# A kernel of linear attention and a mixture of experts: the experts' token lists built by products of one-hot matrices in place of scatters to DRAM

## The chip, the cores and the metric

The kernel runs on one core of one Trainium2 chip. A core has TensorE (PE, matrix products; the load of a weight tile is shown as PEld), VectorE (DVE), ScalarE (ACT), GpSimd (POOL) and SyncE (SP), each with its own instruction stream, and 16 DMA engines that all queues share. The metric is the device time of one execution in microseconds (us), less is better. The three executions of the kernel before took 561.39, 561.18 and 560.62 us, so the median is 561.18 us. The profile is of a further execution that took 574.06 us.

## What is computed

First a delta-rule attention over 768 steps for 4 x 8 heads of 48 features, then a router that sends each of the 3072 tokens to one of 8 experts, a two-layer network each.

```python
for t in range(S):
    kt, vt, bt = (k_n[:, :, t], v[:, :, t], beta[:, :, t, None])
    y[:, :, t] = np.einsum('bhd,bhde->bhe', q[:, :, t], state)
    v_old = np.einsum('bhde,bhd->bhe', state, kt)
    state = state + bt[:, :, :, None] * np.einsum('bhd,bhe->bhde', kt, vt - v_old)
...
logits = x @ w_gate
expert_idx = np.argmax(logits, axis=1)
...
gate_w = probs[np.arange(N), expert_idx]
...
for e in range(E):
    lo, hi = (boundaries[e], boundaries[e + 1])
    h = np.maximum(x_sorted[lo:hi] @ w1[e], 0.0)
    y_sorted[lo:hi] = h @ w2[e]
y = y_sorted[inv_perm]
return (gate_w[:, None] * y).astype(np.float32)
```

Here x is the attention's output, 3072 rows of 384, and the hidden width is 1024. All is in float32.

## The kernel before

**The turns.** The 768 steps are cut into 12 turns of 64 steps. A turn is a chain between PE and ACT: the old state goes through the keys (L558), the residual R is copied out of PSUM, two triangular inverses are applied (L587) with a product across between them (L597), each followed by a copy on ACT, then the state is updated (L611) and copied to S, which starts the next turn. DVE computes the inverses ahead (L441 to L521) and is the busiest engine in the first seven turns. Each turn gives 256 rows of x: `output` (L643) and `logits` (L663, L673, L682) run a turn behind the chain, and x goes to DRAM as `xs`.

**Routing.** The 24 tiles of 128 tokens are handled in five groups: 8, 8, 2, 4 and 2 tiles. `route(m, 0)` finds each token's expert, `route(m, 1)` its rank among that expert's tokens (products with a triangle and with ones, L736 and L740), and from rank and expert a place in a list, `ri`. The entry `ent` is a pair: the token's number (L766) and its gate. For every tile of tokens one indirect DMA of GpSimd (L770) then writes 128 entries of 8 bytes to their places in one of two lists in DRAM, which alternate; both were filled with a large number by two DMAs of 194 KB at about 34 us. There are 24 such scatters.

**Reading the lists.** After groups 0 to 2, that is 18 tiles, the first 256 tokens of expert 0 are known. `early_rows` reads their entries back (`both_e`, L968 takes the minimum of the two lists, L837 makes integers `rows_ei`) and GpSimd gathers the rows from `xs` (L840), while the last two turns still run. `early` then computes these 256 rows: transposes L900, first layer L918, second layer L947, after the last turn. After group 4, `entries` reads the rest (six DMAs on SP to `both_l`, L866 takes the minimum, L837 makes `rows_i`), and the gathers of all experts follow from it. The 10 DMAs that load the weights of experts 1 and 2 stand behind these six on SP's queue.

**The order.** A planner in Python (class `Plan`) holds a cost, a priority and dependencies for each step, simulates the engines, and so writes one fixed order for each engine. Its `prio` numbers only order the plan; at run time an instruction waits for the data that it reads or overwrites. The planner also puts fillers into PE's idle time (L1084, products with the identity)[...]. Each queue works strictly in its order: what stands behind a waiting instruction waits too.

**The experts.** From about 281 us on, PE goes through the 8 experts with hardly a break (L900, L918, L947), the weights of three experts in a ring (`blkA`, `pA`), and GpSimd scatters the finished rows to the output (L847).

Of the kernel before, what the change touches and what calls it, by code (L numbers as in the profile page):

```python
# [20 lines left out]
NT = S // C  # L21
# [17 lines left out]
OUT, LOG = 0.6, 0.9  # L39
LATER, OUTL = 7, 1.1  # L40
# [149 lines left out]
def _consts():  # L190

    p = np.arange(128)[:, None]
    j = np.arange(128)[None, :]
    rev = np.broadcast_to(E - np.arange(E), (128, E))
    first = np.broadcast_to(np.arange(E), (128, E))
    closed = first + E * EARLY * (first == 0)
    i = np.arange(32)[None, :]
    q = np.arange(64)[None, :]  # L200
    parts = [
        ("rev", rev), ("first", first), ("upper", E * (p < j)), ("ones", np.full((128, 128), E)),
        ("ident", p == j), ("number", p),
        ("later", np.concatenate([p % 64 < q, (p % 64) ^ 32 < q], axis=1)), ("fold", p % 32 == i),
        ("places", np.broadcast_to(E * (CAP + 128 * np.arange((NL - CAP) // 128)), (128, (NL - CAP) // 128))),
        ("closed", closed),
    ]
    at, where = 0, {}
    for name, a in parts:
        where[name] = (at, a.shape[1])  # L210
        at += a.shape[1]
    return np.concatenate([a for _, a in parts], axis=1).astype(np.float32), where
# [3 lines left out]
def tile_kernel(ctx: ExitStack, tc: tile.TileContext, kq, ktok, vtok, betal, wgk, w1, w2, out):  # L216
# [7 lines left out]
    lists = [nc.dram_tensor(f"lists{i}", (E * NL, 2), FP32, kind="Internal").ap() for i in range(2)]  # L224
# [113 lines left out]
    P.op("POOL", 0.6, lambda: nc.gpsimd.memset(empty[:], float(FAR)), w=["empty"], prio=-20)  # L338
    for i in range(2):
        P.op(  # L340
            "SP", 0.6, dma(nc.sync, lists[i].rearrange("(p s) o -> p (s o)", p=128), empty[:]),
            r=["empty"], w=[("lists", i)], prio=-1.1,
        )
# [351 lines left out]
    lgs = [pool.tile([128, TG, E], FP32, name=f"lg{i}") for i in range(2)]  # L695

    def route(m, part):
# [9 lines left out]
        ent, ri = w("ent", (TG, 2)), w("ri", (TG,), I32)  # L707
# [44 lines left out]
        else:  # L752
# [5 lines left out]
        dve(4, lambda: nc.vector.tensor_copy(out=ri[:, 0:n], in_=po[:, 0:n]), [K("po")], [K("ri")], pr)  # L758
# [4 lines left out]
        dve(4, lambda: nc.vector.reciprocal(out=ent[:, 0:n, 1], in_=su[:, 0:n]),  # L763
            [K("su")], [K("ent")], pr)
        for i, t in enumerate(g):
            dve(1, lambda i=i, t=t: nc.vector.tensor_scalar(  # L766
                out=ent[:, i, 0:1], in0=const("number"), scalar1=float(t * 128), scalar2=None,
                op0=OP.add), ["cf"], [K("ent")], pr)
        for i, t in enumerate(g):
            P.op("POOL", 1.0, lambda i=i: nc.gpsimd.indirect_dma_start(  # L770
                out=lists[i % 2], out_offset=bass.IndirectOffsetOnAxis(ap=ri[:, i : i + 1], axis=0),
                in_=ent[:, i, :], in_offset=None, bounds_check=E * NL - 1, oob_is_err=False),
                r=[K("ent"), K("ri")], w=[("lists", i % 2)], prio=pr, lat=2.0)
# [31 lines left out]


    LAST = 3 * E
    both_l = pool.tile([128, 2, LAST + 1 + E, 2], FP32, name="both_l")
    rows = pool.tile([128, LAST + 1 + E, 2], FP32, name="rows")
    rows_i = pool.tile([128, LAST + 1 + E], I32, name="rows_i")  # L810
    both_e = pool.tile([128, 2, 2, 2], FP32, name="both_e")
    rows_e = pool.tile([128, 2, 2], FP32, name="rows_e")
# [15 lines left out]
    def prepare(i):  # L828
        v, k = XIN[i]
        P.op("POOL", 1.4, lambda v=v: nc.gpsimd.memset(v, 0.0),  # L830
             w=k + [("xin", i, t) for t in range(4)], prio=10 if i else 9.5)
        if i:
            return
        dve(2 * (LAST + 1 + E) * 2, lambda: nc.vector.memset(both_l[:], float(FAR)), [], [("both", i, j) for i in range(2) for j in range(3)], 9)

    def ids(o, i, k):
        P.op("DVE", 0.12, lambda: nc.vector.tensor_copy(out=o, in_=i), r=[k], w=[k + "i"], prio=12.4)  # L837
# [14 lines left out]
    def by_place(i):  # L852
        return lists[i].rearrange("(n e) o -> n e o", e=E)

    def entries():

        for i in range(2):
            e, q = nc.sync, "SP"
            late = by_place(i)[EARLY : EARLY + 128, 0:1, :]
            P.op(q, 0.3, dma(e, both_l[:, i, LAST : LAST + 1, :], late), r=[("lists", i)], w=[("both", i, 0)], prio=12.3, lat=2.5)  # L860
            tiles = lists[i][0 : 384 * E].rearrange("(p x) o -> p x o", p=128)
            rest = by_place(i)[384:CAP]

            P.op(q, 0.3, dma(e, both_l[:, i, 0:LAST, :], tiles), r=[("lists", i)], w=[("both", i, 1)], prio=12.3, lat=2.5)
            P.op(q, 0.3, dma(e, both_l[0:32, i, LAST + 1 :, :], rest), r=[("lists", i)], w=[("both", i, 2)], prio=12.3, lat=2.5)
        P.op("DVE", 0.13, lambda: nc.vector.tensor_tensor(  # L866
            out=rows[:], in0=both_l[:, 0], in1=both_l[:, 1], op=OP.min),
            r=[("both", i, j) for i in range(2) for j in range(3)], w=["rows"], prio=12.4)
        ids(rows_i[:], rows[:, :, 0], "rows")

    def place(e, t):

        return LAST + 1 + e if t == 3 else LAST if e == 0 else t * E + e

    def fetch(e):
        xv = XIN[e % 2][0]
        allx = [("xs", t) for t in range(2 * NT)]
        for t in (3, 2) if e == 0 else range(4):
            n, c = 32 if t == 3 else 128, place(e, t)
            P.op("POOL", 1.0, lambda t=t, n=n, c=c: gather(xv[0:n, t * DM : t * DM + DM], rows_i[0:n, c : c + 1]),  # L880
                 r=["rowsi", *allx], w=[("xin", e % 2, t)], prio=30 + e, lat=2.5)
# [48 lines left out]
    def finish(on_dve, b, n, gate, idx, k, p):  # L930
# [8 lines left out]
             r=[("bk", b), k], w=[ky], prio=p)  # L939
        P.op("POOL", 1.0, lambda: scatter(y[0:n], idx), r=[ky, k + "i"], w=["out"], prio=p, lat=2.5)  # L940
# [19 lines left out]
    def early_rows():  # L960

        weights(0, 8)
        prepare(0)
        for i in range(2):
            e, q = nc.gpsimd, "POOL"
            P.op(q, 1.0, dma(e, both_e[:, i], lists[i][0 : EARLY * E].rearrange("(p t e) o -> p t e o", t=2, e=E)[:, :, 0, :]),
                 r=[("lists", i)], w=[("both_e", i)], prio=10, lat=2.5)
        P.op("DVE", 0.13, lambda: nc.vector.tensor_tensor(  # L968
            out=rows_e[:], in0=both_e[:, 0], in1=both_e[:, 1], op=OP.min),
            r=[("both_e", 0), ("both_e", 1)], w=["rows_e"], prio=10.5)  # L970
        ids(rows_ei[:], rows_e[:, :, 0], "rows_e")
        xv = XIN[0][0]
        for t in range(2):
            P.op("POOL", 1.0, lambda t=t: gather(xv[:, t * DM : t * DM + DM], rows_ei[:, t : t + 1]),
                 r=["rows_ei"] + [("xs", i) for i in range(18)], w=[("xin", 0, t)], prio=11, lat=2.5)

    def early():
        xT, hT = parts(0, EARLY, 0)
        guard = [k for i in range(3) for k in kKQ(i)]
        turned_rows(0, (0, 1), xT, 20.5, guard)  # L980
        hidden(0, xT, hT, 21, guard, (0, 1, 4, 5))
        for t in range(2):
            second(0, t, hT, 128 * t, 6 + t, 21.2 + 0.01 * t)
            finish(t, 6 + t, 128, rows_e[:, t, 1:2], rows_ei[:, t : t + 1], "rows_e", 21.2)

    def expert(e):
# [23 lines left out]
        def col(t):  # L1010
            c = place(e, t)
            return rows[:, c, 1:2], rows_i[:, c : c + 1]
# [12 lines left out]
    for i in range(NT + AHEAD + 1):  # L1025
        t = i - AHEAD
        for m, g in enumerate(groups):
            if m >= CLOSE and g[-1] == 2 * t - 3:
                route(m, 1)
                if m == CLOSE:  # L1030
                    early_rows()
        if t > 0:
            output(t - 1)
        if 0 <= t < NT:
            load_kv(t)
            turn(t)
        if t > 0:
            logits(t - 1)
            for m, g in enumerate(groups):
                if g[-1] == 2 * t - 1:  # L1040
                    route(m, 0)
                    if t == NT:
                        route(m, 1)
                elif m < CLOSE and g[-1] == 2 * t - 3:
# [9 lines left out]
    entries()  # L1054
    early()

    weights(1, 20, ["rows"])
    weights(2, 21, ["rows"])
    fetch(0)
    fetch(1)  # L1060
    for e in range(E):
# [23 lines left out]
        pairs[pair][:, 0, DM:], lhsT=const("ident"), rhs=const("ident"), start=False, stop=True, skip_group_check=True)  # L1085
# [4 lines left out]
    both_o = pool.tile([128, 2, 2], FP32, name="both_o")  # L1090
    idx = pool.tile([128, 2], FP32, name="idx")
    idx_i = pool.tile([128, 1], I32, name="idx_i")
    flag = nc.values_load(any_i[0:1, 0:1], min_val=0, max_val=E * NM)  # L1093
    with tc.If(flag > 0):
        with tc.For_i(0, E, 1) as ev:
            nt = nc.values_load(more_i[0:1, ds(ev, 1)], min_val=0, max_val=NM)
            with tc.If(nt > 0):
# [5 lines left out]
                with tc.For_i(0, nt, 1) as tv:  # L1103
                    for i in range(2):
                        nc.sync.dma_start(
                            out=both_o[:, i : i + 1, :],
                            in_=lists[i][CAP * E :].rearrange("(t p e) o -> p e t o", p=128, e=E)[
                                :, ds(ev, 1), ds(tv, 1), :].rearrange("p e t o -> p (e t) o"),
                        )
                    nc.vector.tensor_tensor(out=idx[:], in0=both_o[:, 0], in1=both_o[:, 1], op=OP.min)  # L1110
                    nc.vector.tensor_copy(out=idx_i[:], in_=idx[:, 0:1])
# [13 lines left out]
                    for f in range(NF):  # L1125
# [4 lines left out]
                        out=ys[0][:], in0=bk[3][:, 0:DM], scalar1=idx[:, 1:2],  # L1130
# [48 lines left out]
```

## Time and profile before

| what | value |
|---|---|
| median of three executions | 561.18 us |
| the profiled execution | 574.06 us |
| its span, first to last instruction | 572.3 us |
| TensorE's mean granted clock | 0.908 |
| PE busy over the span | 493.6 us (86%) |
| DVE busy | 220.5 us (39%) |
| ACT busy | 196.3 us (34%) |
| POOL busy | 116.4 us (20%) |
| the 24 scatters to the lists (L770), POOL busy | 29.6 us |
| the 134 fillers (L1084), PE busy | 26.9 us |

A group of the page reads: line, engine, operation, output <- input, shapes, count, then busy time and mean duration in ns, then the engine's idle time before these instructions with what ended it. In the timeline a line reads: start, duration, engine, line, operation, count, and in brackets the idle time before it and its releaser. A line with a count above 1 is several instructions merged. "issue" as a releaser means that the engine waited for nothing that the profile shows; "remote" that the semaphore's increment was not matched to an instruction of this core.

### The profile page before, as it was taken

Reading aid. Unit: us, or ns where it says so; the run is one execution under the profiler, and the core shown is the slowest. Engines: PE = TensorE matmul, PEld = TensorE weight load, DVE = VectorE, ACT = ScalarE, POOL = GpSimd, SP = SyncE. Lnnn points to the kernel's source line nnn. Section 1 sums busy time; section 2 is a strip of 40 time slices with the busy share of each in tenths; the row PEclk is TensorE's granted clock in tenths of the full one; section 3 lists DMA queues with packets and bytes.
Section 4 is the critical chain, followed back from the end, with each engine's and each line's share of the span. In section 5 each row is a group of like instructions: output and inputs, shape, how many; then the busy total and the mean of one; then the engine's idle time right before and its main releaser. Section 6 shows DMA issues by size and latency. Waiting matters only on the chain. (4 is left out here: it accounts for less than half of the span.)

```text
span 572.3 us, 15859 instructions
## 1 busy us (share of the span) xinstructions
PE 493.6 (86%) x6854; PEld 339.3 (59%) x6855; DVE 220.5 (39%) x910; ACT 196.3 (34%) x459; POOL 116.4 (20%) x118
## 2 busy tenths in 40 slices
PE   6577888889879884889599999999999999999980
PEld 4466777778767764777465555555554555555540
DVE  5999989997997220041110011001111011101100
ACT  4575978878847722420011111011110110111100
POOL 9000000000162025134430033210133101002011
PEclk8558999979979975899799999999999999999995
DMA  8995464454412450106944244243423400001000
GB/s 203 240 251 156 136 145 122 117 147 114 124 58 68 139 188 4 57 31 230 337 154 124 111 137 135 84 140 111 137 86 124 147 1 27 17 1 43 0 27 14
DMA packets 29641, 64.21 MB, mean 112 GB/s; under 512 B 5558, under 2 KB 18022, under 8 KB 29536
## 3 DMA queue, kind: packets, MB, share of 16 engines
q1 hardware_dynamic: 24336, 52.89, 30.6%
q0 software_dynamic: 4416, 9.47, 4.9%
q8 instruction: 54, 0.88, 0.7%
q10 hardware_dynamic: 816, 0.81, 0.6%
q14 instruction: 19, 0.16, 0.1%
HBM read 49.62 MB, written 11.43 MB: 107 GB/s over the span
## 5 line engine op out<-in xcount | busy, mean ns | idle before, releaser
L918 PE MATMUL pair<-kqA,blkA 128*128 128x416 f32 (+2 forms) x288 | 88.0, 467 | 0.3 <-DVE kqA L908 0.3
L947 PE MATMUL pair<-blkA,kqA 128*128 128x384 f32 x240 | 79.9, 489 | 0.0
L918 PEld LDWEIGHTS pair<-kqA,blkA 128*128 128x128 f32 x288 | 54.6, 201 | 31.6 <-issue 29.3
L924 DVE TENSOR_SCALAR kqA<-pair 128x416 f32<-128x416 f32 (+2 forms) x36 | 19.6, 544 | 132.7 <-PE pair L918 80.1
L847 POOL DMA_INDIRECT out<-y,rows_i x30 | 28.8, 960 | 201.7 <-ACT y L938 144.0
L947 PEld LDWEIGHTS pair<-blkA,kqA 128*128 128x128 f32 x240 | 44.9, 190 | 34.5 <-issue 5.3
L927 ACT ACTIVATE kqA<-pair 128x416 f32<-128x416 f32 (+2 forms) x36 | 17.3, 480 | 114.4 <-PE pair L918 70.5
L918 PE MATMUL pair<-kqA,pA 128*128 128x416 f32 x144 | 51.4, 514 | 0.0
L938 ACT ACTIVATE y<-pair,rows 128x384 f32<-128x384 f32 x15 | 8.7, 582 | 123.1 <-PE pair L947 108.4
L378 PE MATMUL pair<-kqA 48*64 48x128 f32 (+1 forms) x896 | 38.6, 331 | 14.3 <-ACT pA L306 6.4
L534 ACT ACTIVATE v<-v,nt 128x48 f32<-128x48 f32 x192 | 49.2, 331 | 4.2 <-DVE X L502 2.6
L947 PE MATMUL pair<-pA,kqA 128*128 128x384 f32 x144 | 48.0, 490 | 0.0
L935 DVE TENSOR_SCALAR y<-pair,rows 32x384 f32<-32x384 f32 (+1 forms) x15 | 8.5, 607 | 92.3 <-PE pair L1008 88.3
L378 PEld LDWEIGHTS pair<-kqA 48*64 48x64 f32 x896 | 31.6, 182 | 20.5 <-issue 8.2
L587 PE MATMUL pair<-R,blkA 32*32 32x48 f32 x1536 | 30.7, 231 | 12.9 <-ACT R L306 10.4
L918 PEld LDWEIGHTS pair<-kqA,pA 128*128 128x128 f32 x144 | 27.1, 190 | 23.2 <-issue 22.6
L770 POOL DMA_INDIRECT lists<-ent,ri x24 | 29.6, 1235 | 53.1 <-DVE ent L766 21.1
L947 PEld LDWEIGHTS pair<-pA,kqA 128*128 128x128 f32 x144 | 26.9, 190 | 21.2 <-issue 3.8
L558 PE MATMUL pair<-S,kqA 112*64 112x96 f32 x704 | 36.4, 258 | 3.3 <-issue 1.7
L840 POOL DMA_INDIRECT kqA<-xs,rows_i x30 | 29.8, 993 | 35.0 <-PE pair L900 21.7
L587 PEld LDWEIGHTS pair<-R,blkA 32*32 32x32 f32 x1536 | 26.6, 147 | 17.3 <-ACT R L306 11.5
L558 PEld LDWEIGHTS pair<-S,kqA 112*64 112x64 f32 x704 | 31.7, 143 | 6.2 <-issue 4.1
(126 smaller groups left out, 649.4 us busy)
## 6 DMA issues: line engine op xcount, KB each, us to landing
kqA<-in_kq SPq DMA_DIRECT2D x46, 192.0 KB
blkA<-in_w SPq DMA_DIRECT2D x15, 512.0 KB
blkA<-in_w SPq DMA_DIRECT2D x10, 768.0 KB
v<-in_vtok SPq DMA_DIRECT2D x12, 384.0 KB
kt<-in_ktok SPq DMA_DIRECT2D x12, 384.0 KB
xs<-x SPq DMA_DIRECT2D x12, 384.0 KB
pA<-in_w SPq DMA_DIRECT2D x9, 512.0 KB
pA<-in_w SPq DMA_DIRECT2D x6, 768.0 KB
```

The costliest lines, as they stand in the source:

```text
L378: nc.tensor.matmul(bk[bank + e][half(x), i * w : i * w + w].rearrange("p (k c) -> p k c", c=C), lhsT=v[feat(e), 0, x * FQ + f, :], rhs=v[f ...
L534: P.op("ACT", 0.225, lambda v=v, i=i: nc.scalar.activation(out=v, in_=v, func=AF.Copy, scale=nt[:, 16 * u + i : 16 * u + i + 1]), r=[("nt" ...
L558: nc.tensor.matmul(bk[bank + g][half(x ^ g if first else x), 2 * D * i : 2 * D * i + 2 * D], lhsT=KQ(t)[0 : 64 + D, k, x * FQ + f, :], rhs ...
L587: nc.tensor.matmul(at(BZ, f, e)[quad(q)], lhsT=tt[quad(q), :, 16 * u + 8 * e + f], rhs=R[quad(q), f, e, :], start=True, stop=True, skip_gr ...
L770: P.op("POOL", 1.0, lambda i=i: nc.gpsimd.indirect_dma_start(out=lists[i % 2], out_offset=bass.IndirectOffsetOnAxis(ap=ri[:, i : i + 1], a ...
L840: nc.gpsimd.indirect_dma_start(out=dst, out_offset=None, in_=xs, in_offset=bass.IndirectOffsetOnAxis(ap=idx, axis=0), bounds_check=N - 1, ...
L847: nc.gpsimd.indirect_dma_start(out=out, out_offset=bass.IndirectOffsetOnAxis(ap=idx, axis=0), in_=src, in_offset=None, bounds_check=N - 1, ...
L918: nc.tensor.matmul(bk[b][:, 0:n], lhsT=a1[:, s, f * 128 : f * 128 + 128], rhs=xT[:, s, :], start=(s == 0), stop=(s == NK - 1))
L924: (lambda f=f, b=b: nc.vector.tensor_scalar(out=hT[:, f, :], in0=bk[b][:, 0:n], scalar1=0.0, scalar2=None, op0=OP.max))
L927: (lambda f=f, b=b: nc.scalar.activation(out=hT[:, f, :], in_=bk[b][:, 0:n], func=AF.Relu)),
L938: (lambda: nc.scalar.activation(out=y[0:n], in_=bk[b][0:n, 0:DM], func=AF.Copy, scale=gate)),
L947: nc.tensor.matmul(bk[b][:, 0:DM], lhsT=hT[:, f, at : at + 128], rhs=a2[:, f, :], start=(f == 0), stop=(f == NF - 1))
```

## The change

The lists no longer go through DRAM. Each token's place is split into a partition (rank modulo 128) and a column (rank divided by 128, times 8, plus the expert, so 32 columns). DVE builds two one-hot matrices for each tile of tokens: 128 x 128 for the partition, and 128 x 32 for the column, the latter multiplied by the pair (number plus one, gate), which gives 128 x 64. A product of the two on PE, summed in PSUM over the tiles, is the list itself: partition by column, with 0 where no token stands. Three calls of the new function `listed` do this: for the 18 tiles of groups 0 to 2 (into bank BY), for the four of group 3 and for the two of group 4; the sums are put together in `lst` in SBUF. `numbered` turns numbers into row indices: minus one, and a large number where there is none. `early_rows` and the gathers now take their indices from `lst`. The two scatter lists, their fill, the reads back, and the per-tile instruction for the number are gone from the main path; one list and 24 scatters remain inside the branch that handles an expert with over 416 tokens, at the program's end.

In the new order, the 18 products of the first list stand on PE inside turn 10 (six groups of three, between L597, L587, L611, L663 and L558 of before), and the other six inside `early`'s first layer. On SP the 10 weight loads stand directly behind the last write of `xs`. On POOL the gather of expert 1's last 32 rows stands ahead of `early`'s first output scatter, no longer behind it; the gather of the early rows stands ahead of turn 10's write of `xs`, no longer behind it. A few of the planner's numbers change too: the outputs and the logits of a turn get other priorities, the early transposes as well.

```diff
-OUT, LOG = 0.6, 0.9
-LATER, OUTL = 7, 1.1
+OUT, LOG = 0.8, 0.5
+LATER, OUTL = 7, 1.3
+LISTS, L3, L4, TURN = 8.5, 20.2, 11.05, 10.5
...
-    P.op("POOL", 0.6, lambda: nc.gpsimd.memset(empty[:], float(FAR)), w=["empty"], prio=-20)
-    for i in range(2):
-        P.op(
-            "SP", 0.6, dma(nc.sync, lists[i].rearrange("(p s) o -> p (s o)", p=128), empty[:]),
-            r=["empty"], w=[("lists", i)], prio=-1.1,
-        )
...
-        for i, t in enumerate(g):
-            dve(1, lambda i=i, t=t: nc.vector.tensor_scalar(
-                out=ent[:, i, 0:1], in0=const("number"), scalar1=float(t * 128), scalar2=None,
-                op0=OP.add), ["cf"], [K("ent")], pr)
-        for i, t in enumerate(g):
-            P.op("POOL", 1.0, lambda i=i: nc.gpsimd.indirect_dma_start(
-                out=lists[i % 2], out_offset=bass.IndirectOffsetOnAxis(ap=ri[:, i : i + 1], axis=0),
-                in_=ent[:, i, :], in_offset=None, bounds_check=E * NL - 1, oob_is_err=False),
-                r=[K("ent"), K("ri")], w=[("lists", i % 2)], prio=pr, lat=2.0)
+        dve(n, lambda: nc.vector.reciprocal(out=ent[:, :, 1], in_=su[:, 0:n]), [K("su"), "ents"], [("ent", m)], pr)
+
+    def listed(ms, b, pr):
+        a, z = groups[ms[0]][0], groups[ms[-1]][-1] + 1
+        n = z - a
+        i = a > 0
+        key, at, plc = keys_i[:, a:z], places_i[:, a:z], places_f[:, a:z]
...
+        for c in range(a, z, 3):
+            k = min(3, z - c)
+            o, v = ones_p[c // 3 % 2], vals[c // 3 % 2]
+            ko, kv = ("ones_p", c // 3 % 2), ("vals", c // 3 % 2)
+            dve(128 * k, lambda c=c, k=k, o=o: nc.vector.tensor_tensor(
+                out=o[:, 0:k], in0=const("along").unsqueeze(1).to_broadcast([128, k, 128]),
+                in1=places_f[:, c : c + k].unsqueeze(2).to_broadcast([128, k, 128]), op=OP.is_equal),
+                ["cf", ("plc", i)], [ko], pr)
+            dve(32 * k, lambda c=c, k=k: nc.vector.tensor_tensor(
+                out=ones_k[:, 0:k], in0=const("along")[:, 0:32].unsqueeze(1).to_broadcast([128, k, 32]),
+                in1=keys_f[:, c : c + k].unsqueeze(2).to_broadcast([128, k, 32]), op=OP.is_equal),
+                ["cf", ("keyf", i)], ["ones_k"], pr)
+            dve(64 * k, lambda c=c, k=k, v=v: nc.vector.tensor_tensor(
+                out=v[:, 0:k], in0=ones_k[:, 0:k].unsqueeze(3).to_broadcast([128, k, 32, 2]),
+                in1=ents[:, c : c + k].unsqueeze(2).to_broadcast([128, k, 32, 2]), op=OP.mult),
+                ["ones_k"] + [("ent", m) for m in ms], [kv], pr)
+
+            def products(c=c, k=k, o=o, v=v):
+                for x in range(k):
+                    nc.tensor.matmul(
+                        bk[b][:, 0:64], lhsT=o[:, x], rhs=v[:, x].rearrange("p k o -> p (k o)"),
+                        start=(c + x == a), stop=(c + x == z - 1), skip_group_check=True)
+            P.op("PE", 0.27 * k, products, r=[ko, kv], w=[("bk", b)], prio=pr, passes=2 * k, use=128 * k)
+        flat_list = lst[:].rearrange("p k o -> p (k o)")
+        dve(64, (lambda: nc.vector.tensor_tensor(out=flat_list, in0=bk[b][:, 0:64], in1=flat_list, op=OP.add))
+            if i else (lambda: nc.vector.tensor_copy(out=flat_list, in_=bk[b][:, 0:64])),
+            [("bk", b)], ["lst"], -75)
+
+    def numbered(o, of, k, r, pr):
+        n = of.shape[1]
+        far = fars[:, 0:n]
+        dve(n, lambda: nc.vector.tensor_scalar(
+            out=far, in0=of, scalar1=0.0, scalar2=float(FAR), op0=OP.is_equal, op1=OP.mult), r, ["fars"], pr)
+        dve(n, lambda: nc.vector.scalar_tensor_tensor(
+            out=o, in0=of, scalar=-1.0, in1=far, op0=OP.add, op1=OP.add), r + ["fars"], [k], pr)
...
-    entries()
+    numbered(rows_i[:], lst[:, :, 0], "rows_i", ["lst"], -74)
     early()
 
-    weights(1, 20, ["rows"])
-    weights(2, 21, ["rows"])
+    weights(1, 20, ["rows_i"])
+    weights(2, 21, ["rows_i"])
```

## The prediction, made before the changed kernel ran

> **What bounds the kernel now.** I read the slices by time first, then the windows of the turns, then the timeline of the turn that stood out, then the timeline of the passage to the experts.
>
> ```profile
> core 0: us, PE busy (x) PEld busy (x) DVE busy (x) ACT busy (x) POOL busy (x), PEclk, DMA share, GB/s
> 150.00:175.00 25.00, 20.23 (x511) 17.33 (x513) 24.86 (x121) 15.70 (x41) 12.77 (x7) 0.80 0.24 79
> 175.00:200.00 25.00, 22.20 (x788) 19.64 (x784) 12.18 (x61) 18.24 (x46) 2.61 (x3) 1.00 0.31 99
> 200.00:225.00 25.00, 15.23 (x309) 12.52 (x302) 3.00 (x23) 5.67 (x11) 11.26 (x12) 0.66 0.34 113
> 300.00:400.00 100.00, 98.66 (x348) 54.77 (x347) 11.54 (x20) 11.64 (x22) 16.72 (x17) 1.00 0.36 121
> ```
>
> The experts (300 to 400) are bound by PE and aren't touched. In 200 to 225 nobody is busy: PE runs 309 instructions where 25 us before it ran 788, at a clock of 0.66, and DVE and ACT idle. The only engine doing more is POOL, which scatters.
>
> ```profile
> 184.28 1.62 ACT L306 ACTIVATE S<-pair 64x768 f32<-64x768 f32 x2 [1.13 <-PE pair L611]
> 198.35 1.62 ACT L306 ACTIVATE S<-pair 64x768 f32<-64x768 f32 x2 [1.17 <-PE pair L611]
> ...
> 209.08 0.63 PE L587 MATMUL pair<-R,blkA 32*32 32x48 f32 x18 [0.38 <-issue]
> ...
> 215.00 0.28 PE L597 MATMUL pair<-Z,blkA 32*32 32x48 f32 x1 [0.38 <-issue]
> ...
> 221.68 0.97 POOL L770 DMA_INDIRECT lists<-ent,ri  x1 [0.32 <-issue]
> 222.41 0.81 ACT L306 ACTIVATE R<-pair 128x768 f32<-128x768 f32 x1 [11.84 <-remote]
> ...
> 228.31 1.62 ACT L306 ACTIVATE S<-pair 64x768 f32<-64x768 f32 x2 [2.65 <-PE pair L611]
> ```
>
> The copy of S marks a turn. One takes 198.35 - 184.28 = 14.07 us, the next 228.31 - 198.35 = 29.96. The product across (L597) ends at 215.28; the ACT copy that waits for it begins at 222.41, just as the last scatter is being made. PE breaks within one product, where no semaphore is waited for. An earlier turn shows the same: S at 148.60 and 168.72, 20.12 us, with eight scatters from 156.93 to 176.9 and L597 in pieces. The queues in 206 to 223:
>
> ```profile
> q1 hardware_dynamic: 945, 1.40, 22.4%
> q0 software_dynamic: 288, 0.01, 1.4%
> q8 instruction: 1, 0.02, 0.4%
> ```
>
> The weights (q1) end at about 210; then only q0 moves, so bandwidth isn't the cause, and a single page of instructions came in on q8, about what PE used then (some 140 products and as many weight loads).
>
> At the passage:
>
> ```profile
> 259.33 2.74 SPq L293 DMA_DIRECT2D both_l<-lists  x6
> 262.11 0.42 SPq L293 DMA_DIRECT2D pA<-in_w  x1
> 264.28 0.18 DVE L837 CAST rows_i<-rows 128x33 int32<-128x33 f32 x1
> 264.74 0.96 POOL L840 DMA_INDIRECT kqA<-xs,rows_i  x1 [5.34 <-DVE rows_i L837]
> ...
> 274.45 1.02 POOL L847 DMA_INDIRECT out<-y,rows_ei  x1 [3.49 <-ACT y L938]
> 275.78 0.93 POOL L840 DMA_INDIRECT kqA<-xs,rows_i  x1 [0.31 <-issue]
> 281.13 0.48 PE L900 MATMUL pair<-cf,kqA 128*128 128x128 f32 x1 [4.92 <-DMA kqA<-xs,rows_i]
> ```
>
> The early rows' second layer ends at 263.07 + 10.48 = 273.55; the next expert's first layer starts at 281.40. PE waits for the gather of expert 1's last 32 rows, issued at 275.78 because it stands behind the scatter at 274.45, and landing among 5.5 MB of weights (356 GB/s in 262 to 282) that start only at 262.11, behind the six reads of the lists.
>
> **What the Trainium skill says.** "DMA: Bandwidth & Descriptors", section "Anatomy of one DMA — SWDGE (gpsimd) path", gives a DMA from GpSimd about 2 us fixed, mostly completion. The trace agrees: the last scatter is issued at 258.42 to 259.39 and the entries reach `rows` at 264.03, two such latencies. "SBUF — State Buffer", section "Who interferes with whom", says that PE and ACT never wait on anyone, while DVE with two SBUF inputs can meet GpSimd. The trace differs as far as cause can be read from it: between 157 and 169 DVE runs on and PE and ACT stop. "Runtime: NRT & Kernel Launch", section "Instruction fetch mechanics", says that instructions arrive in pages of 256 over a DMA queue; the pages in the trace (209, then 224) don't explain a wait that ends at 222.41. So the stall is tied to the scatters by coincidence in time in two places, not by a known mechanism.
>
> **The change part by part.**
>
> *Scatters out of turn 10.* Without them the turn should be like the one before, 14.07 us, plus what it keeps or gains. It keeps the ranks (L736, L740) ahead of L587, which starts 8.66 us after S instead of 6.01: +2.65. It gains the list. DVE per group of three: 384, 96 and 192 elements; TENSOR_TENSOR takes 419 ns for 256, 692 for 512, 261 for 96, 365 for 192, so 0.55 + 0.26 + 0.37 = 1.18 us, six groups 7.1 us, and five small integer operations of 0.17 before them. DVE is idle there (3.00 of 25 us). Integer shifts aren't in the trace; I take the 0.16 us of the other small ones, and their whole doubling would cost 0.8. PE: 18 products at the 276 ns of L736 (128x64) are 5.0 us; they replace fillers (14 in this turn, 0.20 us each on average, 2.8 us) and idle time. But they stand in order inside the chain. Following the chain with DVE as feeder, the first six delay the second L587 by 0.9 us and the next six delay L611 by 0.7: +1.6, bounded by 0 (hidden) and 12 (each of six groups waits a full 1.18 on DVE and runs its 0.83 on the chain). So 14.07 + 2.65 + 1.6 = 18.3 for 29.96: -11.7.
>
> *Scatters out of turn 7.* Two turns together take 33.1, 31.7, 32.9 and then 35.7 us (from the S copies): against the mean of the first three, 32.55, -3.1. DVE bounds here, so nothing follows behind.
>
> *Last turn.* R to R takes 9.14 us, where it took 5.7 (188.00 to 193.70); the early gathers (235.64, 237.05) lie in it. They move to turn 10, since their indices come sooner and no write of `xs` stands before them. I take 0, between -3.4 and +2.6 (ACT's delay at these gathers).
>
> *The passage.* `rows_i`: before, `ri` at 256.68, then scatters, reads, minimum, 264.46. After, some ten DVE operations of about 0.2, three products queued behind 2.7 us of first layer, a sum and two operations: about 262. The weights stand directly behind the last write of `xs` (247.9), so they start 14 us sooner and are through before the second layer ends; expert 1's last gather is issued with the others at about 269, 4 us before PE needs it. Transposes alone take 1.9 us, so of 281.40 - 273.55 = 7.85 us, 5.95 go. If the gather still met the weights, nothing would go. The six products on PE cost 6 x 0.276 = 1.66. Net -4.3. Next late is PE itself.
>
> *Small.* The fill of the lists (0.4 MB at 34 us, in a stretch where DVE bounds), 24 L766 (0.141 each) and the other constants: 0, with 1 us either way. The reordering of outputs and logits leaves PE's sequence in turns 0 to 9 as it was: 0, with 1.5 us either way.
>
> Sum: -11.7 - 3.1 - 4.3 = -19.1, the profiled execution from 574.06 to 555.0. The median stands 12.9 us below the profiled execution. The experts run at 98.7% PE and can hardly be slower under the profiler, so much of the 12.9 lies in the turns, perhaps in these very stalls. I therefore count the two stalls (14.8) at two thirds to the whole: gain 14.2 to 19.1, on the median 542 to 547. I take 544.
>
> **The rivals.** *B, the stalls are mostly the profiler's, or the two thirds return elsewhere.* For it: the 12.9 us, and no mechanism. Against it: POOL's own waits for its scatters (3.64 at 212.17). The passage and under half the stalls remain: 561.2 - 4.3 - 4 = 553. *D, the passage doesn't close*, because earlier weights collide with the last `xs` write and the gathers: the stalls alone, 561.2 - 12.3 = 549. *C, slower: PE's strict order in turn 10.* If each group of products waits for DVE on the chain, +12 us; with the stalls not real outside the profile that leaves 561.2 + 12 - 4.3 = 569, and it decides once the chain's loss exceeds 4.3 us plus whatever of the stalls is real. Against it: one-hots have two buffers, and DVE has nothing else to do. *The list doesn't leave the path at all* (all effects cancel): 561.
>
> **How the numbers follow.** Forecast 544: 0.56. B 553: 0.26. D 549: 0.09. C 569: 0.06. No change: 0.03. A difference under 0.2% (1.1 us) counts as none. Faster 0.91, same 0.03, slower 0.06. Range: the forecast's own is 540 to 548; below it, 535 takes in the last turn's 3.4 us and the small items, above it B's far end, 556.
>
> **What would show it.** Right: S to S in turn 10 at 17 to 19 us with ACT's R copy following L597 within 0.3 us; two turns around 168 in about 32.5; L587 and L597 unbroken; the weights of experts 1 and 2 issued right behind the last `xs` write; PE's pause after the early second layer under 2.5 us; and the experts from there to the end the same 276 us (281.4 to 557.3). Wrong: ACT waiting "remote" in turn 10 still, which would clear the scatters; PE idle before the new products for DVE on the chain; a pause at the passage for a gather; or a profile 19 us shorter with the median moving by under 10, which is B.

## The result, and the profile after

The changed kernel took 552.59 us (median of four executions, 550.58 to 554.24), the kernel before 560.9 us (four, 560.43 to 561.39). The ratio is 0.985, with a 95% interval of 0.9811 to 0.9889. The gain is 8.3 us where 17 were forecast. The profiled execution of the changed kernel is one of the four, at 554.24 us, so between the two profiled executions the gain is 19.8 us, where the forecast's sum said 19.1. That contradiction is the main thing to explain. Medians here are of all executions of a run, while a ratio and its interval leave out executions over 1.5% above the fastest of the same kernel.

First a window of the changed kernel; the columns are as in the windows shown before.

```profile
core 0: us, PE busy (x) PEld busy (x) DVE busy (x) ACT busy (x) POOL busy (x), PEclk, DMA share, GB/s
200.00:225.00 25.00, 24.26 (x600) 22.38 (x592) 7.82 (x31) 9.60 (x15) 2.20 (x2) 0.80 0.24 83
```

From 200 to 225, PE is now busy for 24.26 us instead of 15.23 and runs 600 instructions instead of 309. POOL's scatters are gone. Turn 10 on ACT's timeline:

```profile
191.71 1.62 ACT L307 ACTIVATE S<-pair 64x768 f32<-64x768 f32 x2 [1.17 <-PE pair L606]
...
202.96 0.81 ACT L307 ACTIVATE R<-pair 128x768 f32<-128x768 f32 x1 [1.40 <-PE pair L592]
...
210.45 1.62 ACT L307 ACTIVATE S<-pair 64x768 f32<-64x768 f32 x2 [3.20 <-PE pair L606]
```

The turn takes 210.45 - 191.71 = 18.74 us, and the copy of R waits for a product (1.40 us), no longer for something remote (11.84 us). The passage to the experts on PE's timeline (L938 is the first layer, L967 the second, L920 the transposes):

```profile
242.74 5.40 PE L938 MATMUL pair<-kqA,blkA 128*128 128x256 f32 x24
251.25 1.09 PE L920 MATMUL pair<-cf,kqA 128*128 128x128 f32 x4 [3.11 <-DMA kqA<-xs,rows_i]
252.13 11.62 PE L967 MATMUL pair<-blkA,kqA 128*128 128x384 f32 x32
263.58 0.82 PE L920 MATMUL pair<-cf,kqA 128*128 128x128 f32 x6
264.24 0.71 PE L938 MATMUL pair<-kqA,blkA 128*128 128x160 f32 x4
```

The pause of 7.85 us behind the early rows' second layer is gone: the second layer ends at 263.75 and the next expert's first layer starts at 264.24. But ahead of the second layer stands a new wait, 3.11 us, of transposes of the same gathered rows: the planner put four of them there.

The next table cuts the spans at the same events. The second column is a later profiled execution of the kernel before, in set 2 of the runs below. The last column is the best version found, described under the last experiment. Each column is one execution.

| from the event before to | before, 574.06 us | before, 558.40 us | after, 554.24 us | best version, 546.73 us |
|---|---|---|---|---|
| the first copy of R | 29.68 | 30.20 | 33.52 | 30.28 |
| the copy of S that starts turn 7 | 118.92 | 116.13 | 116.98 | 117.53 |
| the copy of S that starts turn 10 | 49.75 | 45.03 | 41.21 | 41.43 |
| the next copy of S (turn 10) | 29.96 | 17.07 | 18.74 | 17.91 |
| the last copy of R | 12.72 | 10.23 | 13.77 | 13.05 |
| the early rows' first layer | 11.13 | 17.23 | 11.06 | 10.51 |
| the next expert's first layer | 29.24 | 30.80 | 28.96 | 25.78 |
| the end | 290.90 | 290.01 | 288.26 | 288.41 |
| span | 572.3 | 556.7 | 552.5 | 544.9 |

### The profile page after: what moved, and what is told of

Read it like the earlier page. It is cut to its first block, busy times and chain, and to the rows that moved or that the text cites. A ratio compares the mean times of both kernels' runs of the same rounds, so it can differ in the third digit from the quotient of the medians.

```text
span 552.5 us, 15891 instructions
## 1 busy us (share of the span) xinstructions
PE 483.8 (88%) x6900; PEld 332.0 (60%) x6901; DVE 229.9 (42%) x932; ACT 195.5 (35%) x459; POOL 84.8 (15%) x91
## 5 line engine op out<-in xcount | busy, mean ns | idle before, releaser
L938 PE MATMUL pair<-kqA,blkA 128*128 128x416 f32 (+2 forms) x288 | 86.3, 457 | 0.4 <-DVE kqA L928 0.4
L967 PE MATMUL pair<-blkA,kqA 128*128 128x384 f32 x240 | 81.0, 495 | 0.0
L938 PEld LDWEIGHTS pair<-kqA,blkA 128*128 128x128 f32 x288 | 51.8, 190 | 32.0 <-issue 29.3
L967 PEld LDWEIGHTS pair<-blkA,kqA 128*128 128x128 f32 x240 | 45.5, 193 | 35.0 <-issue 6.4
L373 PE MATMUL pair<-kqA 48*64 48x128 f32 (+1 forms) x896 | 35.4, 305 | 20.2 <-ACT pA L307 12.2
L958 ACT ACTIVATE y<-pair,lst 128x384 f32<-128x384 f32 x15 | 8.7, 581 | 124.2 <-PE pair L967 109.5
L938 PE MATMUL pair<-kqA,pA 128*128 128x416 f32 x144 | 51.4, 514 | 0.0
L967 PE MATMUL pair<-pA,kqA 128*128 128x384 f32 x144 | 48.0, 490 | 0.0
L955 DVE TENSOR_SCALAR y<-pair,lst 32x384 f32<-32x384 f32 (+1 forms) x15 | 8.5, 607 | 92.3 <-PE pair L1023 92.3
L373 PEld LDWEIGHTS pair<-kqA 48*64 48x64 f32 x896 | 28.6, 162 | 26.6 <-ACT pA L307 14.1
L938 PEld LDWEIGHTS pair<-kqA,pA 128*128 128x128 f32 x144 | 27.1, 190 | 23.2 <-issue 22.6
L967 PEld LDWEIGHTS pair<-pA,kqA 128*128 128x128 f32 x144 | 26.9, 190 | 21.2 <-issue 3.8
L582 PE MATMUL pair<-R,blkA 32*32 32x48 f32 x1536 | 28.7, 223 | 4.7 <-ACT R L307 3.3
L582 PEld LDWEIGHTS pair<-R,blkA 32*32 32x32 f32 x1536 | 25.2, 146 | 8.6 <-ACT R L307 4.6
L489 DVE TENSOR_TENSOR prod<-blkA 128x16 f32<-128x16 f32 (+7 forms) x96 | 28.0, 292 | 0.0
```

The costliest lines, as they stand in the source:

```text
L373: nc.tensor.matmul(bk[bank + e][half(x), i * w : i * w + w].rearrange("p (k c) -> p k c", c=C), lhsT=v[feat(e), 0, x * FQ + f, :], rhs=v[f ...
L489: dve(16 * w, lambda j=j, w=w, pl=pl: nc.vector.tensor_tensor(out=pl, in0=gl[:, 16:32, j : j + 1].to_broadcast([128, 16, w]), in1=u[:, j : ...
L582: nc.tensor.matmul(at(BZ, f, e)[quad(q)], lhsT=tt[quad(q), :, 16 * u + 8 * e + f], rhs=R[quad(q), f, e, :], start=True, stop=True, skip_gr ...
L938: nc.tensor.matmul(bk[b][:, 0:n], lhsT=a1[:, s, f * 128 : f * 128 + 128], rhs=xT[:, s, :], start=(s == 0), stop=(s == NK - 1))
L958: (lambda: nc.scalar.activation(out=y[0:n], in_=bk[b][0:n, 0:DM], func=AF.Copy, scale=gate)),
L967: nc.tensor.matmul(bk[b][:, 0:DM], lhsT=hT[:, f, at : at + 128], rhs=a2[:, f, :], start=(f == 0), stop=(f == NF - 1))
```

## The experiments

They ran in four sets, each on another chip and at another time, so that chip and time can't be told apart. The kernel before ran in every set; its medians were 573.30, 558.74, 558.87 and 559.57 us in sets 1 to 4. This spread is a result of its own.

### The scatters put back

Set 1. The changed kernel, with 24 scatters to lists that nobody reads beside the new lists:

```diff
+        for i, t in enumerate(g):
+            P.op("POOL", 1.0, lambda i=i: nc.gpsimd.indirect_dma_start(
+                out=spare_l[i % 2], out_offset=bass.IndirectOffsetOnAxis(ap=ri[:, i : i + 1], axis=0),
+                in_=ent[:, i, :], in_offset=None, bounds_check=E * NL - 1, oob_is_err=False),
+                r=[("ent", m), ("ri", m)], w=[("spare_l", i % 2)], prio=pr, lat=2.0)
```

> The changed kernel with the 24 scatters put back at their old places on GpSimd, to two lists that nobody reads; all other engines keep their order. Theory 1 (the scatters stall PE and ACT by themselves): turn 10 longer than 18.7 us with PE broken within products, 6 to 12 us slower than the changed kernel, about 560 us. Rival 2 (scatters cost nothing in ordinary executions; the gain came from the passage to the experts and from reading the lists sooner): within 2 us of the changed kernel, about 553 to 555 us, with the early gathers later but hidden.

It took 579.26 us (573.08 to 580.83), 27.1 us more than the run without scatters in this set that is nearest to the changed kernel (552.19, the weights held back, below). Its ratio to the kernel before is 1.0105 (1.0058 to 1.0152). Turn 10 took 224.64 - 200.71 = 23.93 us. PE's timeline at the end of that turn:

```profile
220.08 0.35 PE L607 MATMUL pair<-Z,kt 64*48 64x48 f32 x9 [0.18 <-issue]
220.83 0.31 PE L607 MATMUL pair<-Z,kt 64*48 64x48 f32 x5 [0.40 <-issue]
```

and ACT's:

```profile
224.64 1.62 ACT L308 ACTIVATE S<-pair 64x768 f32<-64x768 f32 x2 [6.04 <-remote]
```

The broken products and the remote wait are back with the scatters, although no engine needs what they write. In turn 10 PE breaks eight times within the inverses and the state update here, and once in the changed kernel (0.73 us, at 205.51). So the scatters make the stalls, and since the other five executions are longer still than the profiled one (573.08), the stalls aren't the profiler's.

The size was not foreseen: 27 us where 6 to 12 were expected. How it divides can be read only between the two profiled executions, 573.08 us here and 551.88 with the weights held back. Turn 10 is 7.1 us longer and turns 7 to 9 are 5.5; the stretch from the early rows' first layer to expert 0 is 2.4 longer, where the gathers behind `rows_i` stood behind the last scatters and PE waited 6.72 us for one at 267.11. The start is 2.1 longer, and the rest is spread.

### The kernel before, run again as it is

Sets 1 and 2.

> The kernel before, unchanged, for a second trace. Theory 1 (the profiled execution of 574.06 us was an unusually long one, with stalls that the timed executions of 561 us do not have or have shorter): a span of about 559 us, turn 10 at 20 us or less instead of 29.96, and the difference to the first trace of some 12 us in the turns with scatters. Rival 2 (recording itself lengthens this kernel's stalls whenever it is recorded): a span of about 572 us again, turn 10 again near 30 us, while the timed median stays at 561.

> The kernel before once more. So far it took 560.9 us in one set of runs and 573.3 in another, the changed kernel and its variants about 552 in both. Theory 1 (the scatters' stalls are as long as the chip at hand makes them, the rest of the kernel is not touched by it): whatever the time here, the difference between this trace and the first lies in turns 7, 8 and 10, where the scatters are; near 561 us, turn 10 is 20 us or less, near 573 us it is about 30. Rival 2 (the whole chip is faster or slower): all stages, the experts too, scale together.

Set 1: 571.62 us, and 575.20 for the profiled execution, with turns 7 and 10 at 19.11 and 29.69 us and ACT waiting 8.92 us remote, as in the first profile. Both expectations had the timed executions near 560 us, and both missed that. Set 2: 558.77 us, and theory 1 of that run held. Its profiled execution took 558.40 us, and on ACT's timeline turn 10 is whole:

```profile
191.36 1.62 ACT L306 ACTIVATE S<-pair 64x768 f32<-64x768 f32 x2 [2.64 <-PE pair L611]
...
204.38 0.81 ACT L306 ACTIVATE R<-pair 128x768 f32<-128x768 f32 x1 [2.12 <-PE pair L597]
...
208.43 1.62 ACT L306 ACTIVATE S<-pair 64x768 f32<-64x768 f32 x2 [1.05 <-PE pair L611]
```

17.07 us, with the same scatters in it, PE's inverses and state update in one piece and 0.97 us of POOL for each scatter as before. Between the two sets turns 7 to 10 differ by 18.0 us and the spans by 16.7. So the same scatters stop the chain in one set of runs and not in the other, and the program takes 572 or 559 us by that. What the scatters cost where they stop nothing is on POOL's timeline of set 2's execution:

```profile
218.41 0.97 POOL L770 DMA_INDIRECT lists<-ent,ri  x1 [0.30 <-issue]
220.74 1.52 POOL L293 DMA_DIRECT2D both_e<-lists  x2 [1.35 <-DMA lists<-ent,ri]
225.67 1.10 POOL L840 DMA_INDIRECT kqA<-xs,rows_ei  x1 [3.41 <-issue]
```

and PE's:

```profile
228.91 0.45 PE L900 MATMUL pair<-cf,kqA 128*128 128x128 f32 x1 [1.45 <-DMA kqA<-xs,rows_ei]
235.89 4.42 PE L918 MATMUL pair<-kqA,blkA 128*128 128x256 f32 x12 [0.45 <-DVE kqA L908]
```

The last copy of R, which I take as the chain's end, is at 218.66, and only then do the first 18 scatters end. The lists are read back, and the early rows are gathered 7 us after the chain's end. The changed kernel issues that gather 8.4 us ahead of it:

```profile
215.86 1.18 POOL L879 DMA_INDIRECT kqA<-xs,rows_ei  x1 [30.90 <-DVE rows_ei L823]
```

From the last R to the early first layer it is 17.23 us, against 11.06 in the changed kernel. In the first profile the stall hid this: the chain itself was 22.4 us later there, and the same stretch took 11.13.

### The scatters put back, elsewhere

Set 3, where the kernel before took 558.87 us; the same kernel as above.

> The changed kernel with the 24 scatters back, to lists that nobody reads, once more, since the first run fell where the kernel before took 573. Theory 1 (the scatters stop the chain only in some executions; where the kernel before takes 559 to 561 they cost only GpSimd's own time, and so the gathers behind them): if the kernel before takes under 563 here, this one takes 556 to 564, turn 10 takes 17 to 19.5 from one copy of S to the next, and the early rows' gathers are issued late; if the kernel before takes about 573, it repeats 579 with turn 10 over 22. Theory 2 (the scatters always stop the chain, and the kernel before was faster elsewhere for another reason): over 570 and turn 10 over 22 whatever the kernel before takes.

562.67 us (ratio 1.0066, 1.0035 to 1.0096), turn 10 at 16.95 us: the first theory. Against the changed kernel in set 2 (552.88), where the kernel before took the same, the scatters cost 9.8 us, none of it in turn 10. Between the two profiled executions the spans differ by 7.3 us: 4.5 lie between the early rows' first layer and expert 0, 2.6 in the experts (not explained) and 1.6 in turns 7 to 9, while the start is 2.1 shorter. The largest part is seen on POOL's timeline:

```profile
250.58 0.97 POOL L771 DMA_INDIRECT spare_l<-ents,ris  x1 [0.30 <-issue]
251.86 0.96 POOL L885 DMA_INDIRECT kqA<-xs,rows_i  x1 [0.30 <-issue]
```

and PE's:

```profile
256.32 1.09 PE L926 MATMUL pair<-cf,kqA 128*128 128x128 f32 x4 [7.40 <-DMA kqA<-xs,rows_i]
```

The gathers stand behind the last scatter, issued at 251.86 where the changed kernel of set 2 issued them at 244.47, and PE waits 7.40 us where it waited 3.20. The early rows' gather was issued late too, as expected (222.37, where it was 217.32), but that cost nothing: their first layer starts at 236.06, where it was 235.87. So scatters ahead of that gather aren't enough to delay the early rows. In the kernel before, the read back and the steps behind it come on top.

### The copy of the numbers moved

Sets 1 and 4. The changed kernel copies all token numbers from the constants to `ents` in one DVE instruction, planned ahead of the first inverse. Moved behind the second:

```diff
-    dve(24, lambda: nc.vector.tensor_copy(out=ents[:, :, 0], in_=const("numbers")), ["cf"], ["ents"], -2)
...
+        if i == 4:
+            dve(24, lambda: nc.vector.tensor_copy(out=ents[:, :, 0], in_=const("numbers")), ["cf", ("TT", 1, 1)], ["ents"], 3)
```

> The changed kernel with one DVE instruction moved: the copy of the 24 columns of token numbers stands after the second inverse instead of ahead of the first. Theory 1 (that copy waits on DVE for the constants and then for GpSimd's memsets, and so delays the first inverse by about 3.4 us; DVE bounds the first seven turns, so the whole delay is kept): 3 to 4 us faster than the changed kernel, about 549 us, first residual copy at about 30 us instead of 33.5. Rival 2 (DVE makes the delay good before turn 8, because the turns also wait for ACT and PE): within 1 us of the changed kernel, about 552.5 us.

> The changed kernel itself, as the base for the run beside it. Theory (without scatters it has no stall that depends on where it runs): 551 to 554 whatever the kernel before takes.

> The changed kernel with the copy of the token numbers moved behind the second inverse, beside the changed kernel in the same set. Theory (the copy ahead of the first inverse waits for the constants and then for GpSimd's fills, and all turns start later by that): first copy of R at 30.3 to 30.7 for 33.5, time 2.5 to 3.5 below the changed kernel. Rival (the turns have slack that takes up a late start): first copy of R earlier all the same, time within 1 of the changed kernel.

550.04 us in set 1, and in set 4 549.83 beside 552.02 for the changed kernel itself (six executions each): 2.2 us. The intervals of the two ratios overlap (0.9794 to 0.9863, and 0.983 to 0.9928 for the changed kernel), so the size is uncertain; where it comes from is in the traces. DVE's start in the changed kernel:

```profile
10.34 4.55 DVE L700 COPY ents<-cf 128x24 f32<-128x24 f32 x1 [7.58 <-DMA cf<-c_f]
10.43 6.57 DVE L309 COPY blkA<-pair 32x512 f32<-32x512 f32 x4
17.11 1.30 DVE L436 STREAM_TRANSPOSE blkA<-blkA 128x512 f32<-128x512 f32 x2
18.45 0.19 DVE L444 TENSOR_SCALAR ra<-blkA 128x32 uint32<-128x32 uint32 x1
```

and GpSimd's last fill there:

```profile
14.44 0.41 POOL L905 MEMSET folds<- 128x384 f32 x1
```

The copy of 24 elements waits for the constants until 10.34 and then lasts 4.55 us, to 14.89, when GpSimd's row of fills ends (14.85). The first inverse stands behind it. With the copy moved (set 1), L444 starts sooner and is stretched itself, from 0.19 to 2.54 us:

```profile
12.35 2.54 DVE L444 TENSOR_SCALAR ra<-blkA 128x32 uint32<-128x32 uint32 x1
```

In set 4 these waits were shorter: the copy took 2.40 us there, to 12.78, just as the fill before the last two ended (12.74), the first R came at 31.41, and moving the copy brought it to 29.77. So the copy puts off the first R by 1.6 us within set 4, and by 2.9 to 3.8 us if the first profile (33.52) is set against the two kernels with the copy moved (30.58 and 29.77). The expected 2.5 to 3.5 us was missed by a little, probably because the base of set 4 had lost less than the profile that I took it from. The Trainium skill's "SBUF — State Buffer", section "Who interferes with whom", has it that a copy or a tensor_scalar can take the ports that DVE shares with GpSimd, and that then one of the two blocks for the other's whole instruction. The trace agrees: of DVE's instructions here only these two kinds stretched, and their ends lie within 0.05 us of a fill's end.

### The weights held back

Set 1. The ten weight loads put behind `rows_i` on SP, with one small write there that waits for it:

```diff
+    held = nc.dram_tensor("held", (128, 4 * E), I32, kind="Internal").ap()
+    P.op("SP", 0.3, dma(nc.sync, held, rows_i[:]), r=["rows_i"], w=["held"], prio=12.3, lat=2.5)
```

> The changed kernel with the 10 weight loads of experts 1 and 2 held behind the finished list again, by a small copy of the row indices to DRAM ahead of them on SP. Theory 1 (the early start of the weights is what closes the pause at the passage): the gathers land among the weights, PE pauses again by 4 to 6 us, about 557 to 558 us. Rival 2 (the pause closed because the last gather of expert 1 is issued sooner, whatever the weights do; the weights in flight even slow the first gathers in the changed kernel): within 1.5 us of the changed kernel.

552.19 us (ratio 0.9623). The changed kernel itself didn't run in this set; it took 552.88 and 552.02 in sets 2 and 4. The loads started at 239.71, 19.8 us behind the last copy of R, where in the changed kernel it is 6.7 (230.90 after 224.22). PE still waited for the gathered rows ahead of the second layer, and behind it there was still no pause:

```profile
247.55 1.09 PE L920 MATMUL pair<-cf,kqA 128*128 128x128 f32 x4 [3.73 <-DMA kqA<-xs,rows_i]
```

So the early weights explain neither the closed pause nor the new wait. The forecast's step that the weights "start 14 us sooner and are through" was true of the order and worth nothing that these runs can measure. What is left of that step is the other half, the gather of expert 1's last rows, which is now issued with the others (250.34, where it was 275.78); no run tests it alone.

### The new products twice

Set 2, with the changed kernel beside it. Each product of the list is made a second time, into columns that nobody reads:

```diff
+                    nc.tensor.matmul(
+                        bk[b][:, 64:128], lhsT=o[:, x], rhs=v[:, x].rearrange("p k o -> p (k o)"),
+                        start=(c + x == a), stop=(c + x == z - 1), skip_group_check=True)
```

> The changed kernel on the same chip as the kernel before. Theory 1: 550 to 554 us whatever the kernel before takes, so the gain is 8 us where that takes 561 and 20 us where it takes 573. Rival 2: the ratio of 0.985 stays, 565 us where the kernel before takes 573.

> The changed kernel with each of the 24 products of the lists made twice, the second into columns that nobody reads. Theory 1 (in turn 10 the products stand in PE's order on the chain): 18 more at 0.13 to 0.28 us in turn 10 and 6 in the first layer of the early rows, 3 to 5 us slower, turn 10 at 21 to 22 us. Rival 2 (they fill PE's idle time): within 1.5 us of the changed kernel, turn 10 as before.

554.66 us over 16 executions, with a ratio of 0.989 (0.9853 to 0.9928) beside 0.9862 (0.9803 to 0.9921) for the changed kernel, whose 552.88 us lie in the expected 550 to 554. The intervals overlap: what 24 further products add can't be told from nothing. Turn 10 took 18.98 us, where the changed kernel's took 16.90 in this set and 18.74 and 18.11 in two others; the expected 21 to 22 didn't come. One reserve: the output of this kernel contains values that are not numbers, so the second products aren't as harmless as meant. Turn 10's chain reads nothing of the lists, so its length can be compared: 18 further products cost it at most some 2 us. The total is less sure, since the gathers do read the lists.

### Late numbers, and gathers planned at their true latency

Sets 2 and 3. The planner reckons with 2.5 us from a gather's issue to its rows. In the changed kernel's profile the first two were issued at 243.88 and 245.11, and PE got its rows at 251.25. With 6.0 us for the first two experts, and the copy moved as above:

```diff
-                 r=["rows_i", *allx], w=[("xin", e % 2, t)], prio=30 + e, lat=2.5)
+                 r=["rows_i", *allx], w=[("xin", e % 2, t)], prio=30 + e, lat=6.0 if e < 2 else 2.5)
```

> The changed kernel with the token numbers copied late and the gathers of the first two experts planned at 6.0 us instead of 2.5, which puts the four transposes of expert 0 behind the second layer of the early rows. Theory 1 (PE stands 3.1 us at these transposes for a gather that is late, and 3 us more go by the late copy): 5 to 6 us faster than the changed kernel, 546 to 547 us. Rival 2 (the pause only moves behind the second layer): 2 to 3 us faster, as the late copy alone.

> The changed kernel with the late copy of the numbers and the gathers planned at 6.0 us, once more. Theory (its gain over the changed kernel, some 7 us, is in the program, not in the place or hour of the run): 543 to 549, whatever the kernel before takes. Rival (it was favoured by that set of runs): 550 to 553.

545.97 us in set 2 (ratio 0.9735, 0.9677 to 0.9793) and 546.88 in set 3 (0.9801, 0.9751 to 0.9852). The first is 6.9 us below the changed kernel of set 2, where 5 to 6 were expected; in set 3 the changed kernel didn't run, but 546.88 lies below all its medians elsewhere and within the expected 543 to 549. PE at the passage:

```profile
243.41 10.48 PE L967 MATMUL pair<-blkA,kqA 128*128 128x384 f32 x32
253.73 0.60 PE L920 MATMUL pair<-cf,kqA 128*128 128x128 f32 x4
255.78 0.87 PE L920 MATMUL pair<-cf,kqA 128*128 128x128 f32 x6 [1.46 <-ACT kqA L926]
256.49 7.30 PE L938 MATMUL pair<-kqA,blkA 128*128 128x160 f32 x48
```

The transposes now stand behind the second layer, which starts as the first ends and takes 10.48 us instead of the first profile's 11.62. The early rows and the passage take 25.78 us instead of 28.96. The price is 1.46 us for a copy before expert 0.

## Why the prediction was wrong

**The step that failed** is the one from the profile to the median: "I therefore count the two stalls (14.8) at two thirds to the whole". Just ahead of it stands that much of the 12.9 us between the profiled execution and the median lies in the turns, perhaps in these very stalls. If so, the median executions are those *without* most of the stalls, and what the profile has above the median has to come off the sum: 19.1 - 12.9 = 6.2 us, or 555.0. That is also where the sum itself had landed for the profiled execution, and the changed kernel's own profile lies only 1.65 us above its median. I read the 12.9 us rightly and then turned it round. A later execution of the kernel before shows what an execution at the median's time looks like: at 558.40 us its turn 10 takes 17.07 us and its turns 7 to 9 take 45.03, where the first took 29.96 and 49.75. Together these are 17.6 us, more than the whole difference in span of 15.6. The timed executions of the first comparison have no trace; that they were like this one is inferred from their 561 us. And that the corrected 6.2 us lies near the measured 8.3 is in part luck, since the gain is made of other parts, as follows.

**The stalls as such.** For the first profile they were right: turn 10 was to fall by 11.7 and fell by 11.22. Turn 7 was under-sized: the earlier turns, whose mean I took as the mark, carry DVE's heavy load, and turns 7 to 9 fell by 8.5 us, not 3.1. The products in the turn were under-priced: each of the 18 is two instructions in the trace, while the 276 ns that I took were of one, so they took 7.06 us (1.55 + 2.59 + 1.54 + 1.38) where I had 5.0.

**Why there is a gain all the same** where nothing stalls. From the second to the third column of the table the early rows give 6.2 us, because their gather no longer stands behind scatters and reads; turns 7 to 9 give 3.8, the passage 1.8, the experts 1.7. Against this stand the start (3.3), the stretch up to turn 7 (0.9), turn 10 (1.7) and the last turn (3.5), where the new products and their DVE work stand in the chain. These are two single executions: turn 10 of the changed kernel took 16.90, 18.11 and 18.74 us in its three profiles, so that its 1.7 is no firm cost. The sum is -4.2 us for this pair; the medians gave 5.9 in set 2, 7.55 in set 4 and 8.3 in the first comparison. The largest of these gains I couldn't see in the profile that I had: there the stalled chain arrived so late that the early gather was in time.

**The passage** was forecast at -4.3 and gave 0.35 against the first profile (40.37 to 40.02 us from the last R to expert 0, two rows of the table). The pause went, even by more than said (7.85 to 0.49 us where 1.9 was kept), and the six products cost 1.85 us for 1.66. What I missed is that the planner, with 2.5 us for a gather, moved transposes ahead of the second layer, where PE waits 3.11 us, and that the second layer behind this wait takes 11.62 us instead of 10.48. I had the order of the instructions at hand and looked only behind the second layer.

**The small items** were not 0. The copy of the numbers cost 1.6 to 3.8 us at the start, as it waits for the constants ahead of an inverse on the critical path. The last turn, forecast at 0, was -2.06 from R to R against the first profile, but the stretch ahead of its first R grew by 3.1 (3.58 to 6.69). And of the "two such latencies" behind the last scatter, the second is a read on SP's queue, so it says nothing of a DMA from GpSimd.

**The rivals.** B named 553 and its sign in the test: a profile some 19 us shorter with the median moving by under 10. Its time held, its reason half: the stalls aren't the profiler's, since the timed executions of set 1 took 572 us, but they weren't in the median either. The sum behind B's 553 didn't hold, as it had 4.3 us from the passage and nothing from the early rows; that it met the time is in part luck. D, that the passage doesn't close, came true in its size (0.35 us) and not in its reason: holding the weights back changed nothing. C's strict order on PE shows as no more than the 1.7 us of turn 10 and part of the 3.5 behind it.

## What to carry to other kernels

When the profiled execution is much slower than the median, and a stall in it is as long as the difference, subtract that difference from what removing the stall is to bring, before anything else; the sum made against the profile then stands as the forecast for the median too. A removed stall uncovers what ran beside it: follow each other queue (here GpSimd's, from scatter to gather) from the moment at which the chain would have arrived. And in a planned order look at what the planner moved ahead of the step that you expect to gain, and give it the latency that the trace shows.

## What was unexpected of the hardware

The same program took 573.30 us on one chip and 558.74, 558.87 and 559.57 on three others, while the changed kernel took 552.88 and 552.02 on two of these three, and the two kernels without scatters on the first took 552.19 and 550.04. The kernel with the scatters back took 579.26 on the first and 562.67 on one of the others. So the spread goes with the small indirect scatters. The Trainium skill's "SBUF — State Buffer", section "Who interferes with whom", says, in a list on the ports of SBUF, that PE and ACT never wait on anyone; here PE's products broke and ACT waited 6.04 to 11.84 us while scatters ran. Whether that is at SBUF at all, by which path it happens, and why in one set of four, no run here separates; it stays open.

A pause can cost PE more than its length. Expert 0's first layer of 48 instructions starts after the pause of 7.85 us; the windows of the kernel before over the pause and over that layer:

```profile
273.50:281.40 7.90, 1.52 (x11) 1.04 (x10) 0.85 (x2) 0.89 (x2) 4.25 (x5) 0.90 1.06 377
281.40:290.90 9.50, 9.50 (x51) 9.32 (x51) 1.80 (x5) 0.92 (x4) 2.69 (x3) 0.72 0.36 126
```

At a granted clock of 0.72 the layer takes 9.46 us; in the best version, at 1.00, 7.30. In set 2 the kernel before has the same pause (7.84 us), and the layer takes 8.63 us at 0.82. So 1.3 to 2.2 us came on top of the pause, which the forecast didn't count. The early rows' second layer shows it again, by the clock in its window: 10.48 us at 1.00 with no wait ahead of it, 11.62 at 0.90 after the wait of 3.11 us, and 13.00 at 0.80 after 3.08 us in set 1's kernel with the copy moved. It doesn't follow every time: in set 4's, after 2.90 us, it took 10.49 us at 1.00.
